# An attention and two-layer MLP kernel: finer steps in a hand-written order list, its first part written anew

## The chip, the core and the metric

The kernel runs on one core of one Trainium2 chip. The metric is device time in microseconds (us). The kernel before takes 994.7 us in the median of three runs, 994.26 to 994.94.

## The reference

Three stages follow each other. A recurrent attention with decay runs over 768 steps for 4 batches and 8 heads of 48 channels; its output, 3072 tokens of 384 channels, goes through a gated MLP with 1536 inner channels, and that through an MLP with 2048 inner channels and a squared ReLU.

```python
for t in range(S):
    cur = np.einsum('bhd,bhe->bhde', u[None] * kt, vt)
    y[:, :, t] = np.einsum('bhd,bhde->bhe', rt, state + cur)
    state = wt[:, :, :, None] * state + np.einsum('bhd,bhe->bhde', kt, vt)
x = y                                   # as 3072 tokens x 384
gate = 1.0 / (1.0 + np.exp(-(x @ w_gate)))
x = (gate * (x @ w_val)) @ w_out        # 1536 inner channels
h = np.maximum(x @ w_in, 0.0)           # 2048 inner channels
out = (h * h) @ w_out2
```

The weights reach the kernel as 64-bit floating point numbers, everything else as 32-bit ones.

## The kernel before

**Chunks.** The attention is cut into 24 chunks of 128 tokens (6 per batch, taken batch by batch within each of the 6 positions). Four chunks are one group of 512 tokens. Each chunk goes through stages that the code names by letters. S (`st_scan`) forms decay products by two scans on VectorE and scales r and k by them (L368 to L380). B and R (`st_bonus`, `st_bonus2`) form the diagonal term; GpSimd spreads it into a score tile (L424). A (`st_a`) computes scores on TensorE (L451) and copies the upper triangle into the score tile on VectorE (L454). K (`st_kt`) transposes k on TensorE (L435) and ScalarE copies it out. D decays the state, U (`st_u`) adds the chunk's k-v product to it (L486, L493). Y (`st_y`) computes the output (L466, L472) and splits it into a high and a low part, xh and xl, the input of the MLP. G checks the decay's range on ScalarE; L loads a later chunk.

**The low-high pairs.** A 32-bit operand goes to TensorE as a high half (a cast on ScalarE, L74) and a low half (a subtraction on VectorE, L75). One product is three matmuls: high by high, high weight by low x, low weight by high x (`mm3`, L499 to L501).

**Slots.** The first MLP is cut into 12 tiles of 128 inner channels. A slot is one tile for one group: P projects for the gate into bank gv0 (9 matmuls) and takes a sigmoid on ScalarE; Q projects for the value into gv1 and multiplies on VectorE (L534), and ScalarE casts the product to its high half (L535); l forms its low half gl on VectorE (L539); M multiplies by the output weights into three banks acc (9 matmuls).

**Weight tiles.** Each of the 12 tiles arrives as 1152 KB of 64-bit numbers (raw) and is converted on the chip. `Unit` does this in three ticks (T): a shifts (L195), b joins the low word (L204) and runs a range check on ScalarE (L209), c joins the high word (L215) and runs a second check on ScalarE (L220). The tick after c starts with the split into high and low half (`d`, which casts on ScalarE in L74 and subtracts in L75), and then begins the next tile. `Stream` counts the ticks and issues the loads, four tiles ahead.

**The order.** The scheduler leaves the order as written. A list of letters, `START`, holds the order up to the end of the second group (24 slots); `STEADY` repeats per chunk afterwards. Each letter appends its instructions to the queue of each engine it uses, and each engine works through its queue in order. W n puts n filler matmuls on TensorE (L639, no result used). Z, ahead of the first slot, limits the banks that chunk stages rotate through from eight to the three named rot. The loads of chunks 0 to 3, of their tokens (`load_tok`) and of the first three weight tiles are issued ahead of the list, all on SyncE's queue.

Of the kernel before, what the change touches and what calls it, by code (L numbers as in the profile page):

```python
# [5 lines left out]
F32 = mybir.dt.float32  # L6
# [9 lines left out]
DM = H * D  # L16
# [22 lines left out]
    S0 s0 R0 B1 A0 T B2 R1 K0 W10 S1 T U0 S2 G1 Y0 T W6 A1 K1 R2 T W14 A2 G0 L4 K2 T U1 B3 S3 B4 Y1 L5 W20 R3  # L39
    U2 Y2 W10 A3 G3 K3 T W2 Y3 T U3 R4 P0 T Q0 S4 P1 Q1 D4 l0 B5 W4 K4 T A4 T W3 U4 G4 Y4 G2 l1 T S5 T Z W7  # L40
    P2 M0 T T M1 T Q2 l2 T W1 P3 K5 R5 G5 W7 Q3 W3 P4 T D5 T A5 L6 l3 B6 M2 M3 T T T Q4 l4 U5 T P5 Y5 Q5 T P6
    T S6 M4 T Q6 D6 T R6 l5 T l6 W8 K6 P7 L7 M5 A6 T T Q7 M6 T B7 l7 U6 T P8 Q8 T l8 T S7 W4 P9 Y6 T M7 G6 Q9
    R7 D7 T M8 P10 K7 T A7 L8 Q10 l9 U7 T Y7 M9 l10 G7 P11 B8 Q11 M10 l11 M11 S8 P12 Q12 L9 P13 Q13 R8 l12 D8
    A8 P14 M12 l13 Y8 K8 G8 S9 M13 Q14 U8 B9 P15 D9 T l14 L10 B10 Q15 R9 M14 S10 P16 l15 G9 Q16 A9 M15 Y9 P17
    D10 l16 K9 Q17 M16 U9 R10 l17 P18 A10 K10 L11 B11 Q18 P19 M17 Q19 l18 P20 U10 l19 G10 M18 S11 Q20 D11 P21
    Y10 l20 R11 L12 M19 Q21 M20 K11 P22 l21 S12 G11 Q22 P23 A11 M21 U11 l22 Y11 Q23 B12 R12 M22 L13 l23
# [4 lines left out]
    D K P t Q B+ t l G M P t Q A S+ t l t U M P Y t t Q L t l M t R+  # L51
# [16 lines left out]
EARLY = 8  # L68
VW = 64
# [8 lines left out]
def rwkv_moe(tc, att, tok, vt, u, uc, w1, w2, out):  # L78
# [3 lines left out]
    with ExitStack() as ctx:  # L82
# [77 lines left out]
        class Unit:  # L160
# [99 lines left out]

        def w1_unit(f, note=None):
# [11 lines left out]
            return Unit(3 * DM, w1[f], raw, h, split, note)  # L273
# [5 lines left out]
        s1 = Stream([w1_unit(f, f) for f in range(F1)], 4)  # L279
# [175 lines left out]

        def st_y(i, xh, xl, n):
            d = chunk[i]
            a, v, am, s = d["a"], d["v"], d["am"], block[i % 2]
            py = bank().rearrange("p (a b) -> p a b", b=128)
# [16 lines left out]
            cs = slice(C * n, C * n + C)  # L476
            split_hi_lo(nc, xh[:, :, cs], xl[:, :, cs], py[:, 0:KT])

        def st_u(i):
# [3 lines left out]
            pu = bank()  # L483
# [6 lines left out]
            s = state[d["b"]]  # L490
# [87 lines left out]
        xs = {0: new_x(0)}  # L578
# [13 lines left out]
        def to_x(i):  # L592
            st_y(i, *xs[i // 4], i % 4)

        def load(i):
# [4 lines left out]
            S=lambda i: half(i, 0), s=lambda i: half(i, 1), D=st_decay, G=st_guard, A=st_a, K=st_kt, B=st_bonus, R=st_bonus2,  # L600
            Y=to_x, U=st_u, L=load,
        )
        slots = {}

        def slot(i):
            if i not in slots:
                g, f = i // F1, i % F1
                if f == 0 and g + 1 < NG:
                    xs[g + 1] = new_x(g + 1)
                elif f == 0:  # L610
                    xs[g + 1] = load_x2(0)
# [3 lines left out]
        def st_p(i):  # L615
            if i < F1:
                s1.until(3 * i + 3)
            slot(i).proj(0)
            slot(i).sig()

        def st_q(i):
            slot(i).proj(1)
            slot(i).prod()
# [10 lines left out]
        def warm_up(n):  # L634
# [7 lines left out]
            W=warm_up, P=st_p, Q=st_q, l=lambda i: slot(i).low(), M=st_m, Z=banks,  # L642
            T=lambda i: s1.tick(), t=lambda i: s2.tick(), r=lambda i: refill.tick(), F=lambda i: st_flag(),
# [4 lines left out]
        def steady(g):  # L648
# [3 lines left out]
            seq, n = [], dict(P=F1 * g, Q=F1 * g, l=F1 * g, M=F1 * g - 1)  # L652
# [13 lines left out]
        def last():  # L666
            seq = []
            for f in range(F1):
                k = F1 * (NG - 1) + f
                r = ["r", 0] if f else []  # L670
                seq += ["P", k] + (["F", 0] if f == 1 else []) + ["Q", k] + r + ["l", k] + r
# [247 lines left out]
```

## Time and profile before

| what | value |
|---|---|
| median of three runs | 994.7 us |
| the profiled execution, its own time | 995.02 us |
| its span | 993.3 us |
| TensorE busy | 965.6 us |
| VectorE busy | 534.3 us |
| ScalarE busy | 366.8 us |
| GpSimd busy | 102.6 us |
| mean granted TensorE clock | 0.995 |

Engines are PE (TensorE), PEld (its weight loads, beside PE), DVE (VectorE), ACT (ScalarE), POOL (GpSimd) and SP (SyncE, which issues the DMAs). Busy times of engines overlap, so they don't add up to the span. Names in rows are those of the program: a chunk's input is `a`, its tokens `t`, a weight tile before conversion `raw`, during it `h`, after it `w`. An idle time in brackets belongs to the instruction behind it, and the arrow names what that instruction waited for.

### The profile page before, as it was taken

How to read it: one execution, taken by the hardware profiler on the slowest of the kernel's cores; microseconds unless marked ns; L12 is line 12 of the kernel's file. 1: busy time of each engine (PE TensorE's matmuls, PEld its weight loads, DVE VectorE, ACT ScalarE, POOL GpSimd, SP SyncE). 2: the span in 40 equal slices, each digit the busy share in tenths (PEclk: the TensorE clock that was granted, in tenths of full speed). 3: DMA queues.
4: the chain of work that ended last, by engine and by line, in shares of the span. 5: the costliest groups of instructions: out<-in, count | busy, mean ns of one | idle time of the engine just before them, and what ended most of it. 6: DMA issues, size and time to landing. Idle time of an engine off the chain costs nothing.

```text
span 993.3 us, 14960 instructions
## 1 busy us (share of the span) xinstructions
PE 965.6 (97%) x6157; PEld 820.3 (83%) x6157; DVE 534.3 (54%) x802; ACT 366.8 (37%) x687; POOL 102.6 (10%) x100
## 2 busy tenths in 40 slices
PE   4989999999999999999999999999999999999997
PEld 4766778878888888888888889999999999999997
DVE  6998985645777677777632323333333333333332
ACT  1656563322433333333324433333233323332322
POOL 1100011111112111111104530000000000000000
PEclk9899999999999999999999999999999999999999
DMA  9951112204443443345303320010010100100001
GB/s 256 339 226 34 36 56 87 83 28 134 132 161 127 147 161 126 127 159 168 109 20 118 99 85 30 1 64 1 1 64 1 35 30 1 65 1 1 32 1 36
DMA packets 29724, 83.91 MB, mean 84 GB/s; under 512 B 3456, under 2 KB 15072, under 8 KB 28112
## 3 DMA queue, kind: packets, MB, share of 16 engines
q1 hardware_dynamic: 29504, 82.68, 25.6%
q8 instruction: 50, 0.82, 0.4%
q14 instruction: 26, 0.21, 0.1%
q10 hardware_dynamic: 144, 0.20, 0.1%
HBM read 67.13 MB, written 15.73 MB: 83 GB/s over the span
## 4 chain that ended last, share of the span: by engine, by line
PE 87%; DVE 7%; ACT 2%; DMA 1%; issue 1%; SPq 0%; ACTq 0%; DVEq 0%
PE gv L499 12%; PE gv L501 12%; PE gv L500 12%; PE acc L722 5%; PE acc L720 5%; PE acc L721 5%; PE acc L499 5%; PE acc L500 5%; PE acc L501 5%; PE rot L500 3%; PE rot L501 3%; PE rot L499 3%; PE rot L451 2%; PE rot L722 2%; PE rot L721 2%; PE rot L720 2%
## 5 line engine op out<-in xcount | busy, mean ns | idle before, releaser
L499 PE MATMUL gv<-xh,w 128*128 128x512 f32 x432 | 172.6, 399 | 1.3 <-DVE xl L75 0.8
L501 PE MATMUL gv<-xh,w 128*128 128x512 f32 x432 | 168.8, 391 | 1.2 <-DVE w L75 1.2
L500 PE MATMUL gv<-xl,w 128*128 128x512 f32 x432 | 168.5, 390 | 0.0
L711 DVE TENSOR_TENSOR sig<-sig 128x512 f32<-128x512 f32 x96 | 66.4, 692 | 175.0 <-ACT sig L710 175.0
L534 DVE TENSOR_TENSOR sig<-gv,sig 128x512 f32<-128x512 f32 x72 | 49.6, 688 | 116.8 <-PE gv L501 103.7
L499 PEld LDWEIGHTS gv<-xh,w 128*128 128x128 f32 x432 | 81.1, 188 | 21.6 <-issue 3.0
L501 PEld LDWEIGHTS gv<-xh,w 128*128 128x128 f32 x432 | 81.1, 188 | 20.1 <-DVE w L75 2.9
L720 PE MATMUL acc<-w,gh 128*128 128x384 f32 x288 | 96.7, 336 | 0.0
L721 PE MATMUL acc<-w,gh 128*128 128x384 f32 x288 | 96.6, 335 | 0.0
L535 ACT CAST gh<-sig 128x512 fp32r<-128x512 f32 x72 | 44.7, 621 | 138.4 <-DVE sig L534 138.4
L500 PEld LDWEIGHTS gv<-xl,w 128*128 128x128 f32 x432 | 81.2, 188 | 15.6
L74 ACT CAST gh<-sig 128x512 fp32r<-128x512 f32 x96 | 59.6, 621 | 78.9 <-DVE sig L711 78.9
L500 PE MATMUL acc<-gl,w 128*128 128x512 f32 x216 | 84.6, 392 | 2.6 <-DVE gl L539 2.6
L499 PE MATMUL acc<-gh,w 128*128 128x512 f32 x216 | 86.5, 400 | 0.0
L501 PE MATMUL acc<-gh,w 128*128 128x512 f32 x216 | 84.2, 390 | 0.0
L529 ACT ACTIVATE sig<-gv 128x512 f32<-128x512 f32 x72 | 43.0, 597 | 94.3 <-PE gv L501 93.4
L710 ACT ACTIVATE sig<-rot 128x512 f32<-128x512 f32 x48 | 28.6, 597 | 100.7 <-PE rot L501 97.7
L424 POOL TENSOR_SCALAR_AFFINE_SELECT am<-a 128x1024 f32<-128x1024 f32 x22 | 28.5, 1294 | 353.4 <-DVE a L415 236.6
L539 DVE TENSOR_TENSOR gl<-sig,gh 128x512 fp32r<-128x512 f32 x72 | 52.6, 730 | 19.2 <-ACT gh L535 19.2
L710 ACT ACTIVATE sig<-gv 128x512 f32<-128x512 f32 x48 | 28.7, 598 | 77.6 <-PE gv L501 76.1
L501 PE MATMUL rot<-xhs,w 128*128 128x512 f32 x144 | 56.5, 392 | 0.0
L501 PE MATMUL gv<-xhs,w 128*128 128x512 f32 x144 | 56.5, 392 | 0.0
(149 smaller groups left out, 1832.6 us busy)
## 6 DMA issues: line engine op xcount, KB each, us to landing
a<-in_att SPq DMA_DIRECT2D x23, 675.5 KB, 5.7
raw<-in_w SPq DMA_DIRECT2D x12, 1152.0 KB, 12.4
raw<-in_w SPq DMA_DIRECT2D x32, 384.0 KB, 4.0
t<-in_tok SPq DMA_DIRECT2D x16, 640.0 KB, 6.5
w2f<-h SPq DMA_DIRECT2D x32, 192.0 KB, 2.1
h<-w2f SPq DMA_DIRECT2D x32, 192.0 KB, 2.5
x2d<-x2o SPq DMA_DIRECT2D x18, 256.0 KB, 2.1
x2r<-x2d SPq DMA_DIRECT2D x6, 768.0 KB, 4.4
```

The costliest lines, as they stand in the source:

```text
L74: nc.scalar.copy(hi, src)
L499: nc.tensor.matmul(o, w_hi, x_hi, start=start, stop=False)
L500: nc.tensor.matmul(o, w_hi, x_lo, start=False, stop=False)
L501: nc.tensor.matmul(o, w_lo, x_hi, start=False, stop=stop)
L534: nc.vector.tensor_tensor(out=self.s[:, :n], in0=gv[1][:, :n], in1=self.s[:, :n], op=ALU.mult)
L535: nc.scalar.copy(self.gh[:, :n], self.s[:, :n])
L539: nc.vector.tensor_tensor(out=self.gl[:, :n], in0=self.s[:, :n], in1=self.gh[:, :n].bitcast(F32), op=ALU.subtract)
L710: nc.scalar.activation(r, self.h, AF.Relu)
L711: nc.vector.tensor_tensor(out=r, in0=r, in1=r, op=ALU.mult)
L720: nc.tensor.matmul(o, self.gh[:, cs], hi, start=b0, stop=False)
L721: nc.tensor.matmul(o, self.gh[:, cs], lo, start=False, stop=False)
L722: nc.tensor.matmul(o, self.gl[:, cs], hi, start=False, stop=b1)
```

## The change

**Steps.** A, Y and U are split: A keeps the matmuls, C copies the triangle; Y keeps the matmuls, X splits into high and low; U keeps the matmuls, V updates the state. Q is split into Q (matmuls) and q (product and cast). The conversion of a weight tile is split further: ticks a, b, c stay, but the second check is its own letter N, the high half H and the low half E. `Slots` takes the place of `Stream` for these tiles; it no longer ends a conversion by itself.

**Loads.** Chunk 1 moves ahead of chunk 0's tokens, and chunk 2 ahead of chunk 1's, chunk 3 ahead of chunk 2's.

**Lists.** `START` is written anew with these letters. `STEADY` gets the new letters right behind the old ones (`Q q`, `A C`, `U V`, `Y X`).

```diff
-    S0 s0 R0 B1 A0 T B2 R1 K0 W10 S1 T U0 S2 G1 Y0 T W6 A1 K1 R2 T W14 A2 G0 L4 K2 T U1 B3 S3 B4 Y1 L5 W20 R3
...
+    W33 S0 s0 B1 S1 W6 W15 R0 A0 C0 B2 S2 W8 W2 K0 R1 G0 Y0 U0 K1 L4 T V0 R2 U1 V1 X0 G1 A1 T C1 W3 N0 W15 W5 W3
...
-    D K P t Q B+ t l G M P t Q A S+ t l t U M P Y t t Q L t l M t R+
+    D K P t Q q B+ t l G M P t Q q A C S+ t l t U V M P Y X t t Q q L t l M t R+
...
+            def small(self):
+                n, junk = slice(self.note, self.note + 1), self.lo.bitcast(F32)
+                nc.scalar.activation(junk, junk, AF.Relu, bias=1.0, scale=-1.0 / TINY, accum_out=out_s[:, n])
...
-                if self.note is not None:
-                    n, junk = slice(self.note, self.note + 1), self.lo.bitcast(F32)
-                    nc.scalar.activation(junk, junk, AF.Relu, bias=1.0, scale=-1.0 / TINY, accum_out=out_s[:, n])
...
+        class Slots:
...
+            def tick(self):
+                k, part = divmod(self.k, 3)
+                if k >= len(self.u):
+                    return
+                self.k += 1
+                if part == 0:
+                    self.fetch(k + 1)
+                    self.u[k].a()
+                    self.fetch(k + self.ahead)
+                elif part == 1:
+                    self.u[k].b()
+                else:
+                    self.u[k].c()
...
+            def low(self):
+                if self.e < self.k // 3:
+                    self.u[self.e].low()
+                    self.e += 1
...
+            def high():
+                unit.w = w_slot(f)
+                nc.scalar.copy(flat(unit.w[:, 0]), unit.h)
+
+            def low():
+                hi, lo = flat(unit.w[:, 0]), flat(unit.w[:, 1])
+                nc.vector.tensor_tensor(out=lo, in0=unit.h, in1=hi.bitcast(F32), op=ALU.subtract)
...
-        s1 = Stream([w1_unit(f, f) for f in range(F1)], 4)
+        s1 = Slots([w1_unit(f, f) for f in range(F1)], 4)
...
-            pa = [bank().rearrange("p (a b) -> p a b", b=128) for _ in range(2)]
+            pa = d["pa"] = [bank().rearrange("p (a b) -> p a b", b=128) for _ in range(2)]
...
+        def st_mask(i):
+            d = chunk[i]
             for j in range(2):
                 m = mask.bitcast(I32).unsqueeze(1).to_broadcast([128, NP, C])
-                nc.vector.copy_predicated(d["am"][j], m, pa[j])
...
+        def st_x(i):
+            xh, xl = xs[i // 4]
+            cs = slice(C * (i % 4), C * (i % 4) + C)
+            split_hi_lo(nc, xh[:, :, cs], xl[:, :, cs], chunk[i]["py"][:, 0:KT])
...
         load_att(0, True)
+        load_att(1)
+        nc.sync.dma_start(up, uc)
         load_tok(0)
-        nc.sync.dma_start(up, uc)
-        load_att(1)
+        load_att(2, tag=f"w{F1 - 1}")
         load_tok(1)
         s1.fetch(1)
-        load_att(2, tag=f"w{F1 - 1}")
+        load_att(3, tag=f"w{F1 - 3}")
         load_tok(2, tag=f"w{F1 - 2}")
-        load_att(3, tag=f"w{F1 - 3}")
         load_tok(3, tag=f"w{F1 - 4}")
```

Where the instructions stand is shown at three places. The first is VectorE's queue just ahead of the first slot, before the change. Rows `rk` and `cum` to `a` are a chunk's diagonal term, scans and scaling (`a_341` is chunk 4, in the changed kernel `a_329`), `h` is a step of a weight tile's conversion (`raw_166` is tile 1), `w` its low half, `xl` the low half of a chunk's output.

```order
L399 TENSOR_TENSOR rk_369<-a_341 112x512
L75 TENSOR_TENSOR xl_173<-rot_123,xh_172 128x3x128
L75 TENSOR_TENSOR xl_173<-acc_118,xh_172 128x3x128
L454 COPY_PREDICATED room<-mask,acc_119 128x512
L454 COPY_PREDICATED room<-mask,acc_120 128x512
L215 SCALAR_TENSOR_TENSOR h<-raw_166,h 128x1152
L75 TENSOR_TENSOR xl_173<-gv_122,xh_172 128x3x128
L75 TENSOR_TENSOR w_496<-h,w_496 128x1152
```

And there in the changed kernel:

```order
L454 TENSOR_TENSOR rk_508<-a_329 112x512
L423 SCALAR_TENSOR_TENSOR cum<-a_329,inj 112x520
L428 TENSOR_SCALAR inj<-cum 112x4
L429 RECIPROCAL inj<-inj 112x4
L430 SCALAR_TENSOR_TENSOR cum<-a_329,inj 112x520
L435 TENSOR_TENSOR a_329<-a_329,cum 112x1024
L325 TENSOR_TENSOR w_533<-h,w_533 128x1152
L79 TENSOR_TENSOR xl_173<-gv_121,xh_172 128x3x128
L79 TENSOR_TENSOR xl_173<-acc_119,xh_172 128x3x128
L223 SCALAR_TENSOR_TENSOR h<-raw_166,h 128x1152
```

Chunk 4's scans and scaling and tile 0's low half now stand ahead of the last two xl; tile 1's last step stands behind them, and tile 1's low half further down.

The second place is VectorE's queue at the conversion of tile 3 (`raw_209`, `w_695`), before the change. `sig` is the product of a slot, `gl` its low half.

```order
L215 SCALAR_TENSOR_TENSOR h<-raw_209,h 128x1152
L75 TENSOR_TENSOR w_695<-h,w_695 128x1152
L195 TENSOR_SCALAR h<-raw_313 128x1152
L204 SCALAR_TENSOR_TENSOR h<-raw_313,h 128x1152
L215 SCALAR_TENSOR_TENSOR h<-raw_313,h 128x1152
L534 TENSOR_TENSOR sig<-gv_122,sig 128x512
L539 TENSOR_TENSOR gl<-sig,gh 128x512
L75 TENSOR_TENSOR w_729<-h,w_729 128x1152
```

In the changed kernel tile 3 is `raw_335` and `w_738`, and `a_651` is chunk 5:

```order
L223 SCALAR_TENSOR_TENSOR h<-raw_335,h 128x1152
L199 TENSOR_SCALAR h<-raw_431 128x1152
L600 TENSOR_TENSOR sig<-gv_122,sig 128x512
L423 SCALAR_TENSOR_TENSOR cum<-a_651,inj 112x520
L428 TENSOR_SCALAR inj<-cum 112x4
L429 RECIPROCAL inj<-inj 112x4
L430 SCALAR_TENSOR_TENSOR cum<-a_651,inj 112x520
L435 TENSOR_TENSOR a_651<-a_651,cum 112x1024
L325 TENSOR_TENSOR w_738<-h,w_738 128x1152
L600 TENSOR_TENSOR sig<-gv_122,sig 128x512
L208 SCALAR_TENSOR_TENSOR h<-raw_431,h 128x1152
L605 TENSOR_TENSOR gl<-sig,gh 128x512
```

The low half stood right behind the last conversion step; now the next tile's first step, a product and chunk 5's scans stand between the two.

The third place is SyncE's queue, which issues the loads, at its start, before the change (`t` are a chunk's tokens, `raw_156` is tile 0, `a_152` and `a_158` are chunks 1 and 2).

```order
L325 DMA a_144<-in_att 112x512
L337 DMA t_149<-in_tok 128x512
L566 DMA up<-in_uc 112x8
L327 DMA a_152<-in_att 112x1544
L337 DMA t_154<-in_tok 128x512
L176 DMA raw_156<-in_w 128x2304
L327 DMA a_158<-in_att 112x1544
```

In the changed kernel chunk 1 is `a_149`, chunk 2 `a_154`, chunk 3 `a_160`, tile 0 `raw_158`:

```order
L380 DMA a_144<-in_att 112x512
L382 DMA a_149<-in_att 112x1544
L632 DMA up<-in_uc 112x8
L392 DMA t_152<-in_tok 128x512
L382 DMA a_154<-in_att 112x1544
L392 DMA t_156<-in_tok 128x512
L180 DMA raw_158<-in_w 128x2304
L382 DMA a_160<-in_att 112x1544
```

Chunk 1 moved ahead of chunk 0's tokens, and chunk 2 ahead of chunk 1's tokens and of tile 0.

## Rows read from the trace of the kernel before

**Rows 1.** Page, busy us, share of the span, instructions of each engine

```profile
PE 965.6 (97%) x6157; PEld 820.3 (83%) x6157; DVE 534.3 (54%) x802; ACT 366.8 (37%) x687; POOL 102.6 (10%) x100
```

**Rows 2.** Stretches: us, busy us by engine (count), granted clock, DMA share, GB/s

```profile
3.04:47.06 44.02, 32.27 (x372) 26.57 (x372) 36.23 (x50) 17.33 (x39) 4.88 (x4) 0.92 1.02 314
47.37:147.95 100.58, 93.50 (x720) 72.17 (x719) 90.00 (x106) 63.00 (x114) 8.77 (x6) 1.00 0.27 93
147.95:900.00 752.05, 752.05 (x4623) 641.51 (x4622) 377.83 (x600) 258.64 (x490) 87.03 (x78) 1.00 0.24 78
```

**Rows 3.** TensorE waits, 47.3 to 148 us: total, times, longest

```profile
PE acc L500 <- DVE gl L539: 2.6, 2, 1.3
PE gv L501 <- DVE w L75: 1.2, 4, 0.7
```

**Rows 4.** Chain of waits, 60 to 100 us, shares by line

```profile
by line: ACT w L74 14.4%; DVE w L75 13.7%; DVE h L204 13.2%; ACT raw L220 13.0%; DVE h L195 10.9%; ACT raw L209 10.4%; issue 6.1%; DVE h L215 3.2%; DVE cum L375 3.1%; DVE a L380 3.1%; DVE cum L368 2.9%; DVE gl L539 1.5%; DVE sig L534 1.5%; 
```

**Rows 5.** VectorE waits, 0 to 47.3 us

```profile
DVE rk L399 <- DMA a<-in_att: 4.9, 2, 2.6
DVE h L195 <- DMA raw<-in_w: 1.5, 1, 1.5
```

**Rows 6.** VectorE waits, 47.3 to 148 us

```profile
DVE w L75 <- ACT w L74: 5.0, 7, 1.3
DVE gl L539 <- ACT gh L535: 2.7, 2, 1.4
DVE am L454 <- PE rot L451: 1.5, 1, 1.5
```

**Rows 7.** VectorE in order of time: start, us, instruction [idle before]

```profile
11.30 1.26 DVE L399 TENSOR_TENSOR rk<-a 112x512 f32<-112x512 f32 x1 [2.59 <-DMA a<-in_att]
...
44.70 1.34 DVE L215 SCALAR_TENSOR_TENSOR h<-raw,h 128x1152 int32<-128x1152 int32 x1
46.50 0.56 DVE L75 TENSOR_TENSOR xl<-gv,xh 128x384 fp32r<-128x384 f32 x1 [0.45 <-ACT xh L74]
...
52.88 1.23 DVE L368 TENSOR_TENSOR_SCAN cum<-a,inj 112x520 f32<-112x520 f32 x1
...
55.84 1.23 DVE L380 TENSOR_TENSOR a<-a,cum 112x1024 f32<-112x1024 f32 x1
...
73.41 1.36 DVE L75 TENSOR_TENSOR w<-h,w 128x1152 fp32r<-128x1152 f32 x1 [1.28 <-ACT w L74]
```

**Rows 8.** TensorE in order of time

```profile
47.37 0.48 PE L499 MATMUL gv<-xh,w 128*128 128x512 f32 x1
...
57.12 0.61 PE L435 MATMUL rot<-ident,a 112*128 112x112 f32 x4 [0.85 <-DVE a L380]
57.66 1.16 PE L451 MATMUL acc<-a 48*128 48x128 f32 x16
...
63.16 0.94 PE L639 MATMUL rot<-ident 128*128 128x256 bf16 x7
...
93.55 0.67 PE L486 MATMUL rot<-t,kt 128*64 128x48 f32 x16
...
147.95 0.40 PE L499 MATMUL gv<-xh,w 128*128 128x512 f32 x1
```

**Rows 9.** Stretches ahead of the first projection

```profile
0.00:30.00 30.00, 17.45 (x141) 14.72 (x142) 20.33 (x32) 8.65 (x18) 4.11 (x14) 0.91 0.94 285
20.00:24.00 4.00, 0.36 (x6) 0.36 (x8) 3.86 (x6) 0.00 (x0) 0.00 (x0) 1.00 1.03 339
26.00:28.00 2.00, 2.00 (x12) 1.82 (x11) 1.86 (x5) 1.97 (x8) 0.00 (x0) 0.50 1.04 435
30.00:32.00 2.00, 2.00 (x20) 1.47 (x19) 1.99 (x4) 1.21 (x2) 1.60 (x1) 0.70 1.02 424
```

**Rows 10.** Page, DMA issues: count, KB each, us to landing

```profile
a<-in_att SPq DMA_DIRECT2D x23, 675.5 KB, 5.7
raw<-in_w SPq DMA_DIRECT2D x12, 1152.0 KB, 12.4
```

More of the change, by code (lines that the diff above doesn't have):

```diff
@@ L68 @@
 EARLY = 8
+AFTER = 12
 VW = 64
@@ L259, in until, with __init__, fetch, small @@
                     self.tick()
+        class Slots:
+            def __init__(self, units, ahead):
+                self.u, self.n, self.k, self.e, self.ahead = units, 0, 0, 0, ahead
+            def fetch(self, n):
+                while self.n < min(n, len(self.u)):
+                    self.u[self.n].load()
+                    self.n += 1
+            def tick(self):
[11 more added lines that the diff above has]
+                    self.u[k].c()
+            def small(self, k):
+                self.u[k].small()
+            def high(self, k):
+                self.u[k].high()
+            def low(self):
+                if self.e < self.k // 3:
+                    self.u[self.e].low()
+                    self.e += 1
+            def until(self, n):
+                assert self.e >= n
         def w1_unit(f, note=None):
@@ L272, in w1_unit @@
             h = lambda: flat(sb.tile([128, 3, DM], F32, name="h", tag="h", bufs=2))
-            return Unit(3 * DM, w1[f], raw, h, split, note)
+            unit = Unit(3 * DM, w1[f], raw, h, split, note)
+            def high():
[4 more added lines that the diff above has]
+                nc.vector.tensor_tensor(out=lo, in0=unit.h, in1=hi.bitcast(F32), op=ALU.subtract)
+            unit.high, unit.low = high, low
+            return unit
         def w2_unit(i):
@@ L451, in st_a, with st_y @@
                     nc.tensor.matmul(pa[j][:, p], a[r, p, 1], a[r, p, 0], start=True, stop=True)
+        def st_mask(i):
+            d = chunk[i]
             for j in range(2):
                 m = mask.bitcast(I32).unsqueeze(1).to_broadcast([128, NP, C])
-                nc.vector.copy_predicated(d["am"][j], m, pa[j])
-        def st_y(i, xh, xl, n):
+                nc.vector.copy_predicated(d["am"][j], m, d["pa"][j])
+        def st_y(i):
             d = chunk[i]
             a, v, am, s = d["a"], d["v"], d["am"], block[i % 2]
-            py = bank().rearrange("p (a b) -> p a b", b=128)
+            py = d["py"] = bank().rearrange("p (a b) -> p a b", b=128)
             first = d["c"] == 0
@@ L482, in st_u @@
                 return
-            pu = bank()
+            pu = d["pu"] = bank()
             for h in range(H):
@@ L489, in st_u, with st_state @@
                 )
-            s = state[d["b"]]
+        def st_state(i):
+            d = chunk[i]
+            if d["c"] == NC_ - 1:
+                return
+            s, pu = state[d["b"]], d["pu"]
             un = pu[0:PR, 0 : NP * D].rearrange("p (a b) -> p a b", b=D)
@@ L599, in rwkv_moe @@
         stage = dict(
-            S=lambda i: half(i, 0), s=lambda i: half(i, 1), D=st_decay, G=st_guard, A=st_a, K=st_kt, B=st_bonus, R=st_bonus2,
-            Y=to_x, U=st_u, L=load,
+            S=lambda i: half(i, 0), s=lambda i: half(i, 1), D=st_decay, G=st_guard, A=st_a, C=st_mask, K=st_kt, B=st_bonus,
+            R=st_bonus2, Y=st_y, X=st_x, U=st_u, V=st_state, L=load,
         )
         slots = {}
+        order = [(g, f) for g in range(NG) for f in range(F1)]
         def slot(i):
             if i not in slots:
-                g, f = i // F1, i % F1
-                if f == 0 and g + 1 < NG:
+                g, f = order[i]
+                if i == AFTER:
+                    xs[2] = new_x(2)
+                elif g >= 2 and f == 0 and g + 1 < NG:
                     xs[g + 1] = new_x(g + 1)
-                elif f == 0:
+                elif g >= 2 and f == 0:
                     xs[g + 1] = load_x2(0)
@@ L615, in st_p @@
         def st_p(i):
-            if i < F1:
-                s1.until(3 * i + 3)
+            s1.until(order[i][1] + 1)
             slot(i).proj(0)
             slot(i).sig()
-        def st_q(i):
-            slot(i).proj(1)
-            slot(i).prod()
         def st_m(i):
@@ L641, in rwkv_moe @@
         stage.update(
-            W=warm_up, P=st_p, Q=st_q, l=lambda i: slot(i).low(), M=st_m, Z=banks,
-            T=lambda i: s1.tick(), t=lambda i: s2.tick(), r=lambda i: refill.tick(), F=lambda i: st_flag(),
+            W=warm_up, P=st_p, Q=lambda i: slot(i).proj(1), q=lambda i: slot(i).prod(), l=lambda i: slot(i).low(), M=st_m, Z=banks,
+            T=lambda i: s1.tick(), E=lambda i: s1.low(), N=s1.small, H=s1.high, t=lambda i: s2.tick(), r=lambda i: refill.tick(), F=lambda i: st_flag(),
             f=lambda i: st_flag2(),
```

27 lines of the change are left out of this document (13 added, 14 removed).

## Prediction

> **What bounds the kernel now.** I read the page first, then the stretches, the waits of TensorE and VectorE, the chain, and last both engines in order of time. The page gives TensorE 97% of the span [rows 1], so the only time to be won is where it is idle or does filler. The stretches say where that is. From 147.95 us, where the last of the 12 slots of the first token group begins, to 900 us TensorE is busy 752.05 of 752.05 us; from 47.37, where the first projection begins, to 147.95 it is busy 93.50 of 100.58 us; and before 47.37 it has done only chunk work and filler [rows 2, 8]. What stands behind the order list is the same instruction for instruction on all five engines in both programs, so the 845 us after 147.95 cost what they cost now, and the question is when that point is reached.
>
> TensorE waits there for VectorE: for the low half of a gated product (gl, L539), for the low half of a weight tile (w, L75), for a scaled chunk [rows 3]. The chain from 60 to 100 us runs through the conversion of the weight tiles and hardly touches TensorE: casts on ScalarE (L74), the steps on VectorE (L195, L204, L215, L75), two checks on ScalarE (L209, L220) [rows 4]. VectorE is busy 36.23 of the 44.02 us from its first scan to the end of the last xl ahead of the first projection, and 90.00 of the next 100.58 [rows 2]. It is the second full engine, and its own waits count: 4.9 us for chunk inputs and 1.5 for the first weights [rows 5], later 5.0 for the cast of a weight tile, 2.7 for that of a product, 1.5 for scores [rows 6]. The cast wait is built into the order: the low half is queued right behind the step that the cast needs, as at 73.41 us, with 1.28 us idle [rows 7].
>
> **The change part by part.** No arithmetic is added; the same instructions stand in another order, plus 31 filler matmuls (130 for 99). Of these, 126 stand ahead of the first projection (62 before) and 4 behind it (37 before).
>
> *Up to the first projection.* In both programs it waits for the xl of all four first chunks. VectorE's work up to that point is today's 36.23 us [rows 2], plus chunk 4's scans and scaling, which now come first (52.88 to 57.0, 4.1 us), less the last step of weight tile 1, which now comes after (44.70, 1.34 us) [rows 7]: 39.0 us. Its idle time today is 44.02 - 36.23 = 7.8 us. The loads of chunks 1 and 2 move ahead of the tokens of chunk 0 and of the first weights, and tile 0 is converted after chunk 2 rather than between chunks. Chunk 1's wait is 2.59 us (at 11.30). One 256 KB token load no longer stands ahead of it; at the 285 GB/s of the first 30 us [rows 9] that is 0.9 us, so 1.7 us of wait stay. Chunk 2 then has chunk 1's five steps as cover, tile 0 another five, and I cost both waits at nothing; the 0.45 before the xl at 46.50 goes too, since the last two xl now stand behind tile 0's low half. With 0.9 us of small gaps 2.6 us of idle stay. So the last xl ends at 3.04 + 39.0 + 2.6 = 44.6 and the first projection starts 0.3 later as today, at 44.9: **2.5 us earlier**, with chunk 4's scores and transposes already done.
>
> Two bounds for this. If chunk 1's wait goes too, and operations that no longer start after a wait run closer together, as the ones at 52.88 to 57.0 do (1.24 + 0.17 + 0.18 + 1.24 + 1.23 in 4.1), it is 42.5. If instead chunk 4's input is late, every later row of VectorE's queue is: with itself and what stands ahead of it, five chunk loads, four of tokens (256 KB), three weight tiles and one of 192 KB, 8.24 MB must have moved [rows 10], which at 285 GB/s have moved at 28.9 us; with the 5.7 us that such a load takes to land it is there at 34.6, and VectorE wants it at 44.6 less the 7 us of the rows between, 37.6. It is in time by 3 us, not by more; a tenth less bandwidth makes it even. I take 46.5 as the late end.
>
> *From there to slot 11.* TensorE's work today is 93.50 us [rows 2]. The filler that goes is 33 matmuls at 0.94 / 7 = 0.13 us, 4.4 us. Chunk 4's transposes (0.61) and scores (1.16) moved ahead, one state update (0.67) came in [rows 8]: -1.1. That leaves 88.0 us. VectorE's work is 90.00 - 4.1 + 1.3 = 87.2 us from the last xl to the low half of tile 11. So the two engines have the same amount of work between the same two points, and every wait on either shows. What stays of VectorE's 10.6 us of idle there (100.58 - 90.00)? High and low half of a tile are now two entries. For most tiles three or more other operations stand between the last conversion step and the low half, for tile 3 the next tile's first step, a product and a chunk's scans; only tiles 9 and 11 have two and one. So of the 5.0 us I keep 1.0. A product's low half stands one to nine operations behind its product: the 2.7 goes. Masks no longer follow the scores at once: 0.5 of 1.5 stays. I add 0.5 for a late chunk and keep the other 1.4 us of small gaps: 3.4 us. Tile 11 is then ready at 44.6 + 87.2 + 3.4 = 135.2; slot 11 needs it 0.5 us after its start, so it cannot start before 134.7, which is 44.9 + 88.0 + 1.8.
>
> TensorE has waits of its own besides. The split lets a PSUM bank be held from the scores to the masks and from the output to its x, while other work passes, and after the first projection three banks turn over. Chunk 6's scores take the bank that chunk 5's output filled, which VectorE empties only behind chunk 6's scans; chunk 7's transposes do the same with chunk 6. VectorE reaches these reads after 37.2 and 56.4 us of work from the last xl (the durations of its queue in the new order), TensorE reaches the transposes and scores after 37.2 and 57.2 us from the projection, which itself starts 0.3 after that xl. With 1 and 2 us of VectorE's idle by then, TensorE stands there for 0.7 and 0.9 us; the second holds a part of the first: 1.3 us in all. So slot 11 starts at 44.9 + 88.0 + 1.8 + 1.3 = 136.0 in place of 147.95, **11.95 us earlier**. Behind it, chunk 8's scores directly follow slot 11's projections and may wait a further microsecond; I count it in the range. Moved steps of ScalarE (checks, guards) go at nothing: it is busy 63.00 of 100.58 us [rows 2], and is hidden as long as no cast stands behind a sigmoid that waits for TensorE.
>
> The sum against the profiled execution's 995.02 us is 983.1. The median of the runs is 0.3 lower, 994.7, so I predict **982.8 us**.
>
> **The rivals.** *Both engines run full.* Projection at 42.5, bank and cast waits all covered, 0.5 us of idle: 42.5 + 88.0 + 0.5 = 131.0, 17 us earlier, 977.7. For it: enough operations stand between producer and consumer almost everywhere. Against it: two queues of 87 and 88 us that wait for each other a dozen times each.
>
> *VectorE's waits stay, under other names.* With all of its 10.6 us of idle kept, tile 11 is ready at 44.6 + 87.2 + 10.6 = 142.4, and slot 11 starts at 141.9: 6 us earlier, 988.6. With the late projection (46.5) it is 4.5 us, 990.2. For it: the amount of work is unchanged and ScalarE's queue is in order. Against it: 5.0 of the 10.6 us have a known cause which the new order removes.
>
> *The clock falls among the slots, and it is slower.* Filler no longer fills TensorE's waits behind the first projection. Today TensorE is busy 0.36 of the 4 us from 20 to 24 us, and then is granted 0.50 of its clock, the 1.2 GHz level; the stretch from 30 to 32 us shows 0.70, part of it at the 2.4 GHz level [rows 9]. One such episode costs the wait of 4 us, and half of the 7 us that follow it, 7.5 us. From two more than I count (12 + 2 us over 7.5) the kernel is slower than today; three make it 982.8 + 22 = 1005. The place would be a late chunk load, at which VectorE's whole queue stands, weights included. Against it: no wait of today behind 47.37 is over 1.3 us, with the clock at 1.00 throughout [rows 2, 3]. The Trainium skill's rule speaks for this rival (TensorE: Matmul & The Clock Gate, "Why this matters for your kernels": avoid idle gaps between bursts of matmuls, since one of them takes the array back to the lower clock). The trace agrees ahead of the projections, and shows no case behind them.
>
> *It does nothing that can be measured.* The list only trades places: what TensorE gains at the start it waits for later, because VectorE's sum is the bound. VectorE would need 15 to 17 us of idle between the two points, more than today's 10.6.
>
> **How the numbers follow.** My forecast, 979 to 986.5: 0.58. VectorE's waits stay, 986.5 to 991: 0.21. Both full, under 979: 0.13. Nothing measurable (about 0.2%, 2 us, is what this kernel's measurement can tell from no change): 0.04. Slower: 0.04. The range leaves out the nothing, the slower and the outer ends of the second and third: 977.5 to 989.5. Faster 0.92, same 0.04, slower 0.04.
>
> **What would show it.** First projection between 43.5 and 46; the wait of the weight tile's low half for its cast about 1 us in place of 5.0; TensorE's idle time from there to slot 11 about 3 us in place of 7.08; slot 11's start near 136, and the rest of the span as long as now. I am wrong if VectorE still idles 8 us or more between the two points, if a new wait for PSUM or for a chunk's load of over 2 us appears, or if TensorE shows idle time after slot 11.

## The result and the profile after

The changed kernel takes 978.68 us (median of 4 runs, 977.60 to 979.64), the kernel before 994.48 (4 runs, 992.52 to 994.94): a ratio of 0.9845, with a 95% interval of 0.9827 to 0.9862. It is 15.8 us faster. 982.8 was predicted, with a range of 977.5 to 989.5.

| us | before | predicted | after |
|---|---|---|---|
| first projection starts | 47.37 | 44.9 | 44.68 |
| from there to slot 11 | 100.58 | 91.1 | 88.18 |
| slot 11 starts | 147.95 | 136.0 | 132.86 |
| from there to the end of the span | 845.35 | as before | 844.94 |
| profiled execution | 995.02 | 983.1 | 979.64 |

The page of the changed kernel gives the busy time of each engine in us, its share of the span and the number of instructions [rows 1]:

```profile
PE 964.9 (99%) x6188; PEld 824.6 (84%) x6188; DVE 525.3 (54%) x802; ACT 365.7 (37%) x686; POOL 103.8 (11%) x100
```

TensorE's busy time is the same within a microsecond, with 31 more instructions. The span is 15.5 us shorter, and so the gain is idle time of TensorE. The stretches of the changed kernel show where (length, then the busy time of PE, PEld, DVE, ACT and POOL with their counts, granted clock, DMA share, GB/s) [rows 2]:

```profile
3.00:45.09 42.09, 39.66 (x437) 32.79 (x435) 37.83 (x55) 18.16 (x45) 6.43 (x5) 0.88 1.02 312
44.68:132.86 88.18, 85.79 (x681) 69.33 (x681) 86.45 (x102) 60.87 (x104) 13.71 (x9) 1.00 0.38 131
132.86:900.00 767.14, 766.75 (x4702) 656.22 (x4701) 376.64 (x609) 263.84 (x500) 82.15 (x76) 1.00 0.23 75
```

The second row is the one to compare. Idle time there is 88.18 - 85.79 = 2.39 us on TensorE (7.08 before) and 88.18 - 86.45 = 1.73 on VectorE (10.58 before). From slot 11 on TensorE is full, as before.

TensorE's waits in that stretch of the changed kernel (waiting line, what it waited for, us in total, times, longest) [rows 3]:

```profile
PE rot L506 <- DVE xl L79: 1.2, 1, 1.2
PE rot L506 <- DVE a L435: 0.7, 1, 0.7
PE rot L490 <- DVE xl L79: 0.4, 1, 0.4
```

The waits for gl and for the low half of a weight tile are gone. The first and the third row are new; in order of time (start, us, instruction, in brackets the idle time before it) they stand here [rows 8]:

```profile
44.68 0.49 PE L565 MATMUL gv<-xh,w 128*128 128x512 f32 x1
...
83.43 1.16 PE L506 MATMUL rot<-a 48*128 48x128 f32 x16 [1.23 <-DVE xl L79]
...
103.35 0.60 PE L490 MATMUL rot<-ident,a 112*128 112x112 f32 x4 [0.45 <-DVE xl L79]
...
132.86 0.39 PE L565 MATMUL gv<-xh,w 128*128 128x512 f32 x1
```

These are chunk 6's scores and chunk 7's transposes. Each waits until VectorE has read the output of the chunk before it out of the same bank.

VectorE's waits in the same stretch of the changed kernel [rows 6]:

```profile
DVE w L325 <- ACT w L321: 0.8, 3, 0.4
DVE gl L605 <- ACT gh L601: 0.4, 1, 0.4
```

And its waits from 0 to 48 us [rows 5]:

```profile
DVE xl L79 <- ACT xh L78: 2.2, 2, 1.3
DVE cum L423 <- DMA a<-in_att: 1.4, 1, 1.4
DVE rk L454 <- DMA a<-in_att: 1.3, 1, 1.3
```

The second row belongs to the first scan, which waits as long in both kernels. Behind it the waits for loads fell from 4.9 and 1.5 us to the 1.3 of the last row. The first row is a wait that the prediction did not have. The chain from 60 to 100 us has turned round [rows 4]:

```profile
by line: DVE w L325 13.1%; DVE h L208 10.7%; issue 10.0%; DVE h L223 9.4%; DVE cum L423 8.7%; DVE cum L430 6.3%; DVE gl L605 6.1%; DVE sig L600 6.0%; DVE am L512 5.2%; DVE h L199 5.1%; DVE inj L428 4.9%; ACT raw L217 3.5%; ACT w L321 2.9%; 
```

Before, three lines of ScalarE held 38% of it (a cast and two checks). Now they hold under 7%, and the chain runs from one VectorE instruction to the next. VectorE's queue still sets the end of this stretch, but it hardly stands still.

### The profile page after: what moved, and what is told of

It reads as the page before. It is cut to its first block, busy times and chain, and to the rows that moved or that the text cites. A ratio compares the mean times of both kernels' runs of the same rounds, so it can differ in the third digit from the quotient of the medians.

```text
span 977.8 us, 15032 instructions
## 1 busy us (share of the span) xinstructions
PE 964.9 (99%) x6188; PEld 824.6 (84%) x6188; DVE 525.3 (54%) x802; ACT 365.7 (37%) x686; POOL 103.8 (11%) x100
## 4 chain that ended last, share of the span: by engine, by line
PE 84%; DVE 10%; ACT 2%; issue 2%; DMA 1%; SPq 0%; ACTq 0%; DVEq 0%
PE gv L565 11%; PE gv L566 11%; PE gv L567 11%; PE acc L784 5%; PE acc L782 5%; PE acc L783 5%; PE acc L565 4%; PE acc L566 4%; PE acc L567 4%; PE rot L566 3%; PE rot L567 3%; PE rot L565 3%; PE rot L784 2%; PE rot L783 2%; PE rot L782 2%
## 5 line engine op out<-in xcount | busy, mean ns | idle before, releaser
L601 ACT CAST gh<-sig 128x512 fp32r<-128x512 f32 x72 | 44.6, 620 | 132.5 <-DVE sig L600 127.0
L479 POOL TENSOR_SCALAR_AFFINE_SELECT am<-a 128x1024 f32<-128x1024 f32 x22 | 27.8, 1266 | 327.8 <-DVE a L470 198.2
```

Of the source, the lines that this page charges most:

```text
L601: nc.scalar.copy(self.gh[:, :n], self.s[:, :n])
```

## The experiments

My theory: the gain is the time in which VectorE stood at an instruction whose producer on another engine was not done, while work that was ready stood behind it in its queue. The rivals: the first loads carry it; the filler that left TensorE carries it; or the amount of VectorE's work is all that counts, and the order nothing. Every ratio below is to the kernel before, in runs on the same chip; differences in us to the changed kernel (978.68) are across chips, on which the kernel before took 994.5 to 995.5 us.

### The first loads in the old order

```diff
 load_att(0)
-load_att(1); up
 load_tok(0)
-load_att(2)
+up
+load_att(1)
 load_tok(1)
...
+load_att(2)
 load_tok(2)
+load_att(3)
```

> The changed kernel with the old order of the first loads (chunk 0, its tokens, chunk 1, its tokens, tile 0, chunk 2), all else as changed. Theory 1 (the reason given in the prediction, only chunk 1's load gains, by one 256 KB token load): first projection 0.9 to 1.5 us later than the changed kernel's 44.68 us, total 979.5 to 980.5 us. Theory 2 (chunk 2 behind tile 0 matters too, since VectorE wants chunk 2 before tile 0 now): the wait of 2.3 us for chunk 2 comes back as well, first projection 3 us or more later, total 981.5 to 983 us.

Measured: 980.34 us, ratio 0.9846 (0.9825 to 0.9866). The first projection starts at 45.39 instead of 44.68, and the stretch to slot 11 takes 88.16 us instead of 88.18. So the order of the loads is worth 0.7 us of the 15.8 at the first projection (0.9 was the term for it), too little to show in the ratio. The list has the rest. The wait that theory 2 expected does come: VectorE waits 3.8 us for chunk inputs instead of 1.3, 3.0 of it at once. But its 2.2 us for the cast of xh are then gone, so that the projection hardly moves; with that wait removed by other means the loads could be worth more, which no run shows.

### The kernel before, without its late filler

```diff
-... l0 B5 W4 K4 T A4 T W3 U4 ... Z W7 P2 ... T W1 P3 K5 R5 G5 W7 Q3 W3 P4 ... W8 K6 ... W4 P9 ...
+... l0 B5 K4 T A4 T U4 ... Z P2 ... T P3 K5 R5 G5 Q3 P4 ... K6 ... P9 ...
```

> The kernel before without the 37 filler matmuls behind the first projection, all else as before. Theory 1 (as in the prediction's sum, filler is work that goes): 4.4 us less, 990 us. Theory 2 (it only filled waits for VectorE, which last as long without it): TensorE's idle time between first projection and slot 11 grows from 7.08 to 10 us or more, and the time stays within 1.5 us of 994.5. In either the clock could fall behind the first projection; by theory 2 it stays at 1.00, since no wait is over 2.5 us.

Measured: 996.54 us, ratio 1.0011 (0.9998 to 1.0024). Nothing is won. The stretch from the first projection to slot 11 in this kernel, and 25 us of it (columns as above):

```profile
47.97:148.47 100.50, 91.47 (x683) 71.42 (x683) 90.11 (x106) 63.05 (x114) 8.73 (x6) 0.97 0.27 94
...
75.00:100.00 25.00, 22.61 (x167) 17.62 (x168) 21.13 (x24) 17.29 (x30) 1.26 (x1) 0.93 0.09 33
```

TensorE has 37 instructions less than before and idles 9.03 us instead of 7.08; the stretch is as long as it was. The filler had only filled waits for VectorE. The granted clock is 0.93 from 75 to 100 us, where it was 1.00 with the filler, and even that adds nothing to the stretch, since TensorE is not what is waited for. Theory 2 is right on the time and wrong on the clock, which it expected to stay at 1.00.

### The low half back at its step

Only the place of H and E in the list changes (and for tiles 1, 3 and 4 that of the check N), for all but tiles 5, 7 and 11: they stand behind the last step and the check of their tile, ahead of the next tile's first step (tile 3 as the example).

```diff
-... T N3 L6 q1 H3 V3 S5 P2 E Q2 ...
+... T N3 H3 E T L6 q1 V3 S5 P2 Q2 ...
```

> The changed kernel with the cast and the low half of a weight tile back ahead of the next tile's first step, as in the kernel before (tiles 5, 7 and 11 stand so already), so that 0 to 1 us of VectorE work stands between last step and low half in place of 2 to 10 us. Theory 1 (the distance between last step and low half is what took the waits away): VectorE waits for casts of 5 us or more behind the first projection (0.8 in the changed kernel), total 982 to 986 us. Rival (the amount of work and the start decide, the waits move elsewhere): within 1.5 us of the changed kernel, 977.5 to 980 us.

Measured: 1004.26 us, ratio 1.0081 (1.0062 to 1.0100): the whole gain is gone, and more than theory 1 expected (982 to 986). VectorE's longest group of waits up to 180 us in this kernel (0.8 us in the changed kernel), and one of them in order of time:

```profile
DVE w L325 <- ACT w L321: 18.4, 10, 3.8
```

```profile
50.32 1.36 DVE L325 TENSOR_TENSOR w<-h,w 128x1152 fp32r<-128x1152 f32 x1 [1.27 <-ACT w L321]
```

What VectorE has to do between the last step of a tile and its low half was added up for each of the twelve tiles. Where it is nothing (seven tiles in this kernel) VectorE stands for 1.2 to 2.7 us each time; with 0.7 and 1.0 us of work it stands for 3.8 and 1.7; with 1.1 for 0.4, and with 5.8 and 6.1 us not at all. In the changed kernel this work is 1.1 to 6.0 us in tiles 1 to 11, and the three waits are 0.2, 0.2 and 0.4. So the distance is what the list has to give. It has to cover more than the cast itself (1.15 us on ScalarE): at the wait of 3.8 us two checks, a copy and another cast stand ahead of it in ScalarE's queue, and in the kernel before tile 11 waited 0.7 us with 3.3 us of work between.

Two of the ten waits lie ahead of the first projection, which starts at 51.24 instead of 44.68. From there to slot 11 it takes 106.70 us instead of 88.18, and VectorE idles 21.75 of them: about 16 for casts and 3.9 for TensorE. The granted clock is 0.91 there; how much a slower TensorE adds to these waits is not told apart here.

### The split steps joined again

Three kernels: C, X and V directly behind A, Y and U and also q behind Q; only q; only C, X and V. All else in the list keeps its place.

```diff
-... K0 R1 G0 Y0 U0 K1 L4 T V0 R2 U1 V1 X0 G1 A1 T C1 ... P0 Q0 Y4 T N2 L5 E B5 q0 ...
+... K0 R1 G0 Y0 X0 U0 V0 K1 L4 T R2 U1 V1 G1 A1 C1 T ... P0 Q0 q0 Y4 X4 T N2 L5 E B5 ...
```

> The changed kernel with the chunk stages and slots joined again: triangle copy right behind the scores (or behind the diagonal term, where that is later), split of the output right behind the output, state update right behind its matmuls, product right behind the value projection; conversions and loads as changed. Theory 1 (the split of conversions and the new list give the gain, the split of stages little): within 2.5 us of the changed kernel, 978 to 981 us, VectorE waiting 2 to 4 us more on TensorE. Rival (the split of stages carries it): 985 us or more.

Measured: 1016.46 us, ratio 1.0221 (1.0200 to 1.0241), 22 us slower than the kernel before. Theory 1 is out, and the loss is far over the rival's 985 us.

> The changed kernel with only the products joined again: product and its cast right behind the value projection in the list, all chunk stages split as changed. With everything joined the kernel took 1016 us, and VectorE waited 17.6 us for the value projection and 6.6 for sigmoids. Theory 1 (VectorE stands at a product that TensorE has not yet made, with work behind it): most of that comes back here, 990 to 1005 us, VectorE waiting 8 us or more for products. Rival (the chunk stages make it): within 3 us of the changed kernel.

Measured: 1005.85 us, ratio 1.0106 (1.0077 to 1.0135): theory 1, just above its range.

> The changed kernel with only the chunk stages joined (triangle copy, split of the output, state update right behind their matmuls); products stay apart, as changed. Everything joined was 38 us slower than the changed kernel, products alone 27 us. Theory 1 (a joined operation makes VectorE or ScalarE stand ahead of work that is ready): 985 to 995 us, with ScalarE's cast of the output and its copies of the state waiting for TensorE. Rival (the products made nearly all of it): 978 to 982 us.

Measured: 995.89 us, ratio 1.0011 (1.0001 to 1.0020): theory 1, again just above its range.

So the products alone cost 27 us against the changed kernel, the stages alone 17, and both 38, less than the sum. VectorE's waits, first in the kernel with the products joined, 43 to 150 us:

```profile
DVE sig L600 <- ACT sig L595: 8.5, 5, 2.4
DVE sig L600 <- PE gv L567: 6.3, 3, 3.2
```

Then with the stages joined, 0 to 140 us:

```profile
DVE xl L79 <- ACT xh L78: 12.8, 4, 5.5
```

One place of each in order of time, with the instruction behind it. Products joined:

```profile
49.61 0.69 DVE L600 TENSOR_TENSOR sig<-gv,sig 128x512 f32<-128x512 f32 x1 [1.85 <-ACT sig L595]
50.22 1.35 DVE L208 SCALAR_TENSOR_TENSOR h<-raw,h 128x1152 int32<-128x1152 int32 x1
```

Stages joined:

```profile
54.48 0.56 DVE L79 TENSOR_TENSOR xl<-rot,xh 128x384 fp32r<-128x384 f32 x1 [5.47 <-ACT xh L78]
54.95 1.35 DVE L208 SCALAR_TENSOR_TENSOR h<-raw,h 128x1152 int32<-128x1152 int32 x1
```

The changed kernel at the same first product:

```profile
48.45 1.34 DVE L208 SCALAR_TENSOR_TENSOR h<-raw,h 128x1152 int32<-128x1152 int32 x1
49.72 1.34 DVE L325 TENSOR_TENSOR w<-h,w 128x1152 fp32r<-128x1152 f32 x1
50.99 0.67 DVE L454 TENSOR_TENSOR rk<-a 112x512 f32<-112x512 f32 x1
51.59 0.67 DVE L600 TENSOR_TENSOR sig<-gv,sig 128x512 f32<-128x512 f32 x1
```

Joined, the conversion step (L208), whose data are there, stands behind a product that waits 1.85 us for a sigmoid. Split, the step runs first, and the product finds its sigmoid done. That is the theory, shown at both kinds of steps. What these kernels do not show is how good a list without splits could be: this one was written for split steps, and the kernel before, whose list was written for joined ones, is faster than the first two and about as fast as the third.

### No filler ahead of the first projection

```diff
-    W33 S0 s0 B1 S1 W6 W15 R0 A0 C0 B2 S2 W8 W2 K0 R1 G0 Y0 ... C1 W3 N0 W15 W5 W3 ...
+    S0 s0 B1 S1 R0 A0 C0 B2 S2 K0 R1 G0 Y0 ... C1 N0 ...
```

> The changed kernel without the 126 filler matmuls ahead of the first projection; the 4 behind it stay. Theory 1 (VectorE's queue sets the first projection, the filler only passes the time): first projection within 1 us of 44.68 us, total within 1.5 us of the changed kernel. Rival (it holds the clock up for the chunks' small matmuls and the first slots): with a granted clock of 0.5 in parts of the first 60 us, transposes, scores and outputs take twice as long, VectorE waits for them, and the first projection comes 3 to 6 us later, total 981.5 to 985 us. In the changed kernel the clock is 0.50 from 20 to 26 us all the same.

Measured: 979.18 us, ratio 0.9844 (0.9822 to 0.9865): the 126 filler matmuls are worth nothing that can be told. The first projection starts 1.1 us earlier (43.59), and VectorE no longer waits for the cast of xh ahead of it (2.2 us in the changed kernel): of its two parts there, 1.27 us end at 23.32, behind matmuls that ran at 0.50 of the clock, and 0.90 us end at 33.91, behind 26 filler matmuls that held TensorE for 4.58 us from 24.48. The stretch behind takes 88.20 us, as in the changed kernel. The clock ahead of the projection, in this kernel:

```profile
20.00:28.00 8.00, 7.09 (x102) 6.03 (x100) 7.97 (x9) 5.85 (x14) 2.06 (x1) 1.00 1.01 365
28.00:32.00 4.00, 1.33 (x12) 1.27 (x14) 3.86 (x6) 3.37 (x11) 0.87 (x1) 0.85 1.04 340
32.00:36.00 4.00, 3.08 (x43) 2.30 (x41) 4.00 (x8) 0.00 (x0) 1.88 (x1) 0.50 1.02 426
```

And in the changed kernel:

```profile
12.00:16.00 4.00, 2.78 (x30) 2.47 (x26) 3.90 (x6) 1.68 (x5) 1.61 (x2) 1.00 1.06 359
16.00:20.00 4.00, 3.66 (x54) 2.93 (x54) 3.90 (x7) 0.39 (x2) 0.40 (x1) 0.69 0.99 232
20.00:28.00 8.00, 8.00 (x58) 6.73 (x58) 6.69 (x9) 5.76 (x14) 1.15 (x1) 0.52 1.04 384
```

### Less work on VectorE, in both kernels

The step that joins the low word is left out for weight tiles 2 to 11, so that their weights lack their lowest bits.

```diff
-                i = self.h.bitcast(I32)
-                nc.vector.scalar_tensor_tensor(...)
+                if self.note is None or self.note < 2:
+                    i = self.h.bitcast(I32)
+                    nc.vector.scalar_tensor_tensor(...)
```

In the changed kernel:

> The changed kernel without the step that joins the low word (L208) in tiles 2 to 11, 10 operations of 1.27 us on VectorE; the tiles then lack their lowest bits. It asks how much of VectorE's 86.45 us of work between first projection and slot 11 still sets the time. Theory 1 (both engines are full there, TensorE idle 2.3 us): at most 2.5 us less than the changed kernel, 976 to 978.5 us. Rival (VectorE alone is the bound and TensorE would follow): 6 us less or more, below 973 us.

Measured: 975.10 us, ratio 0.9794 (0.9773 to 0.9815).

In the kernel before:

> The kernel before without the same step (L204) in tiles 2 to 11, 12.7 us of VectorE's work; the tiles lack their lowest bits. Theory 1 (its waits come from the order, and from VectorE's amount of work only where the queue is behind): TensorE's 7.08 us of idle between first projection and slot 11 fall to about 4, total 990 to 993 us. Rival (VectorE's amount of work is the bound before, so most of the step's time comes back): 7 us less or more, 988 us or below.

Measured: 986.40 us, ratio 0.9912 (0.9891 to 0.9934). The stretch from the first projection to slot 11, first of the changed kernel with less work, then of the kernel before with less work:

```profile
44.32:129.11 84.79, 84.79 (x681) 69.64 (x681) 76.54 (x93) 60.72 (x104) 13.58 (x9) 1.00 0.41 140
```

```profile
46.87:139.75 92.88, 90.59 (x719) 72.61 (x719) 76.28 (x96) 62.98 (x114) 7.98 (x6) 1.00 0.29 104
```

In the kernel before VectorE has 13.7 us less to do there and slot 11 comes 8.2 us earlier: the rival, by which the amount of VectorE's work was the bound too, was right there. In the changed kernel 9.9 us less bring 3.8 us, between the two expectations, and then TensorE is busy for the whole stretch. So VectorE's sum and its order both set the time before (the kernels with the low half back or with joined steps do the same work as the changed one, and lose 17 to 38 us); after the change TensorE alone lies only 3.4 us under the stretch (88.18 - 84.79).

### The r-k products on GpSimd

A try for a faster kernel: the one without early filler, with a VectorE product per chunk (L454, 0.68 us) handed to GpSimd, which is idle most of the time.

```diff
-                nc.vector.tensor_tensor(out=chunk[i]["rk"][:, ps], in0=a[:, ps, 0], in1=a[:, ps, 1], op=ALU.mult)
+                (nc.gpsimd if i else nc.vector).tensor_tensor(out=chunk[i]["rk"][:, ps], ..., op=ALU.mult)
```

> The changed kernel without the 126 early filler matmuls, and with the r-k products of chunks 1 to 7 (L454, 0.6 us each) on GpSimd in place of VectorE. Theory 1 (VectorE's work sets the first projection, and behind it a part of the time): first projection about 2 us earlier than the 43.59 us without early filler, total 974 to 977 us. Rival (GpSimd's reads hold VectorE back by as much as the 0.6 us that each product frees): first projection at 43 us or later, total 977 to 981 us.

Measured: 982.85 us, ratio 0.9882 (0.9865 to 0.9898), some 4 us slower than the kernel without early filler (979.18, on another chip). The first projection comes at 43.48, no earlier than 43.59, and the stretch grows from 88.20 to 93.52 us. VectorE's groups up to 137 us in this kernel (line, shape, count, busy us, mean ns):

```profile
L208 DVE SCALAR_TENSOR_TENSOR h<-raw,h 128x1152 int32<-128x1152 int32 x12 | 17.2, 1433 | 0.1
...
L430 DVE TENSOR_TENSOR_SCAN cum<-a,inj 112x520 f32<-112x520 f32 x7 | 10.1, 1441 | 0.2
L423 DVE TENSOR_TENSOR_SCAN cum<-a,inj 112x520 f32<-112x520 f32 x7 | 9.7, 1390 | 0.9 <-DMA a<-in_att 0.9
L435 DVE TENSOR_TENSOR a<-a,cum 112x1024 f32<-112x1024 f32 x7 | 9.4, 1342 | 0.7
...
L605 DVE TENSOR_TENSOR gl<-sig,gh 128x512 fp32r<-128x512 f32 x10 | 8.3, 831 | 0.4 <-ACT gh L601 0.4
```

The same groups in the kernel without early filler, from which this one differs by the move alone:

```profile
L208 DVE SCALAR_TENSOR_TENSOR h<-raw,h 128x1152 int32<-128x1152 int32 x12 | 16.9, 1408 | 0.0
...
L435 DVE TENSOR_TENSOR a<-a,cum 112x1024 f32<-112x1024 f32 x8 | 11.2, 1400 | 0.3
L423 DVE TENSOR_TENSOR_SCAN cum<-a,inj 112x520 f32<-112x520 f32 x8 | 10.9, 1369 | 0.0
L430 DVE TENSOR_TENSOR_SCAN cum<-a,inj 112x520 f32<-112x520 f32 x8 | 9.9, 1242 | 0.3
...
L605 DVE TENSOR_TENSOR gl<-sig,gh 128x512 fp32r<-128x512 f32 x10 | 7.2, 723 | 0.4 <-ACT gh L601 0.4
```

Most means are longer by 2 to 16%, one (L435) is shorter by 4%. The means hide that single instructions beside GpSimd's take up to 1.1 us more than the median of their kind while the others keep it; one such pair stands in the last section. Up to 130 us this excess is 8.6 us in all, for 5.0 without the move, so that 3.6 of the 4.2 us that seven products of 0.6 us free are lost again. The rival was right, and the loss is larger than it had it. VectorE's busy time in the stretch, 88.00 us, is higher than without the move (86.41). And TensorE waits 3.2 us for an xl that empties a bank, for which it does not wait at all without the move:

```profile
PE rot L506 <- DVE xl L79: 3.2, 1, 3.2
```

No version with the whole computation was measurably faster than the changed kernel.

## Why the prediction was right, and what was mis-sized

**The place.** Right: of the 15.5 us by which the span shrank, 2.69 lie ahead of the first projection and 12.40 between it and slot 11; the 845 us behind differ by 0.41.

**The first projection.** 44.9 predicted, 44.68 measured, but by luck: three errors cancel. VectorE's work up to the last xl is 37.8 us, not 39.0, and it idles 4.3 us, not 2.6: chunk 1's wait is 1.3 us (1.7 predicted), small gaps 0.8 (0.9), and a wait of 2.2 us for the cast of xh was costed at nothing. So the last xl ends at 45.09, not 44.6. And the projection starts 0.4 us ahead of that end, not 0.3 behind it: its first matmul reads the high half alone, and the first that reads xl starts at 45.14. The wait of 2.2 us goes with the early filler, as the run without it shows. Of the 1.2 us of missing work 0.8 is time in which VectorE was held up beside GpSimd (last section): 1.5 us of it ahead of the projection before, 0.7 after.

**The cast waits.** 5.0 us should have shrunk to 1.0; they are 0.8. The product's low half should have lost its 2.7; 0.4 is left. The reason given was right in kind, too narrow in words: of the seven tiles that waited before, only tile 3 had its low half directly behind its step, the others had 0.6 to 3.3 us of work between. With the distance taken away, the waits come back (18.4 us up to 180 us, 1004.26 us).

**The bank waits.** Predicted at chunk 6's scores (0.7 us) and chunk 7's transposes (0.9, the second holding a part of the first; 1.3 in all). Measured at these two places: 1.23 and 0.45, 1.7 in all. They were the only waits of TensorE that the change added; the third one left, 0.7 us for a scaled chunk, stands for 1.0 before (a row that rows 3 leave out).

**The step that failed in size: from the first projection to slot 11, "TensorE work", 88.0 us.** This term took before's busy 93.50 us for work. The kernel before with less VectorE work runs the same TensorE instructions there (719 recorded for 720) in 90.59 us of busy time, with 2.29 us of idle instead of 7.08. The granted clock is 1.00 in both, so 2.9 us of "busy" went with the waits. With 90.59 in the same sum, 90.59 - 4.4 - 1.1 = 85.1, against 84.79 in the changed kernel with less VectorE work, where TensorE never waits, and 85.79 in the changed kernel itself (87.4 in the two runs whose clock fell for a while, with the stretch as long). The credit of 4.4 us for 33 filler matmuls holds only in this sum; by itself, in the kernel before, the removal was worth nothing (996.54 us), because that filler covered waits.

**VectorE's side** was mis-sized as much, and the sum needs both: by it VectorE held slot 11 until 134.7 us however little TensorE had to do. From the last xl to the low half of tile 11 it has 85.65 us of work (87.2 predicted) and idles 1.73 (3.4 predicted), so tile 11 is ready at 132.47, not 135.2, and the 1.8 us that slot 11 was to wait for it did not come: no wait of TensorE for a weight tile is left in the stretch. Term by term slot 11 comes 0.2 us earlier by the first projection, 2.2 by TensorE's work, 1.8 by tile 11, and 1.1 later by TensorE's other waits (2.39 for 1.3): 132.86 for 136.0.

**The rivals.** *Both engines run full* gave 977.7 and, by its bound of 979, the median of 978.68 falls to it by 0.3 us: the forecast's own 979 to 986.5, given 0.58, was missed by as much. The rival's mechanism is not what happened: the first projection did not come at 42.5, and the bank waits were not covered. Its 88.5 us for the stretch meet the 88.18 by luck, with too much TensorE work and too little waiting. The forecast's mechanism with smaller terms on both engines gives the time. *VectorE's waits stay* is out: 1.73 of 10.58 us stay. *The clock falls* did not happen here (1.00 over the stretch), but its mechanism exists: the granted clock there was 0.97 without the late filler, 0.91 with the low half back at its step, and 0.92 to 0.97 in the three kernels with joined steps. In all of these TensorE waits longer, and how much of their time is the clock's share stays open. A short fall cost nothing: with the old loads and without early filler TensorE idles only 0.74 and 0.83 us in the stretch, the mean clock is 0.98, and the stretch takes 88.16 and 88.20 us. So the changed kernel does not owe its time to a clock of 1.00.

## What to carry to other kernels

When one engine's in-order queue sets the time of a stretch, look for instructions that wait for another engine while ready work stands behind them, split the step there, and put ready work between the two halves, enough for the producer and for what stands ahead of it in its own queue; in this list, which was written for split steps, taking that distance away cost 17 to 27 us for each kind of step, and the costs do not add up. Busy time in a stretch with many waits can hold some cost of the waits, so an estimate of what stays without them takes it too high (93.50 against 90.59 us). Filler that covers a wait can't be counted as a gain when it goes.

## What was not expected of the hardware

Filler did not keep the clock up for long. In the changed kernel TensorE is busy without a break from 2 to 14.8 us, with filler above all, and then stands 1.36 us for a mask. From 18 to 26 us it is granted 0.50 of its clock, the 1.2 GHz level, although it is busy again all the while; over 20 to 28 us that is 0.52 at 8.00 of 8.00 us busy. Without early filler it is busy for 7.09 of the same 8.00 us and is granted 1.00, the 2.4 GHz level. There the fall comes later, 0.50 from 32 to 36 us, behind a stretch of 4 us with only 1.33 busy. What the filler did buy lies at the very start: the same eight matmuls, in the changed kernel, without early filler, and in the changed kernel again while 0.50 was granted:

```profile
10.28 1.02 PE L467 MATMUL rot<-up,rk 112*128 112x2 f32 x8
```

```profile
10.28 1.84 PE L467 MATMUL rot<-up,rk 112*128 112x2 f32 x8 [10.28 <-DMA up<-in_uc]
```

```profile
19.78 1.73 PE L467 MATMUL rot<-up,rk 112*128 112x2 f32 x8
```

The profile gives a granted clock of 1.00 at the first two of these. By the durations that can't be right for the kernel without early filler: its next group of this kind takes 1.73 us too (at 14.87), and only the one at 20.39 us takes 1.06. So its clock column is not to be trusted up to there.

A short wait can be enough for a fall. A wait of TensorE for a scaled chunk (0.71 us without early filler, 0.65 with the old loads) is followed by 4 us at a granted clock of 0.62 (from 64 us) and 0.60 (from 66); the same wait of 0.71 us in the changed kernel is followed by 1.00 (from 65). Why it differs stays open.

Single VectorE instructions are held up while GpSimd works, beside its other instructions (L457, L458, L479) and not only beside the moved products. The moved product of chunk 1, the scan that starts beside it, and the same scan in the kernel without early filler:

```profile
9.53 1.26 POOL L454 TENSOR_TENSOR rk<-a 112x512 f32<-112x512 f32 x1 [6.96 <-DMA a<-in_att]
```

```profile
9.54 2.34 DVE L423 TENSOR_TENSOR_SCAN cum<-a,inj 112x520 f32<-112x520 f32 x1 [0.90 <-DMA a<-in_att]
```

```profile
10.52 1.23 DVE L423 TENSOR_TENSOR_SCAN cum<-a,inj 112x520 f32<-112x520 f32 x1
```

The scan takes its own 1.23 us and most of the product's 1.26. In the first 130 us of all twelve traces every VectorE instruction that is over 0.1 us longer than the median of its kind (kinds with three or more) overlaps one of GpSimd, in the kernel before too: 80 of them, 3 to 11 in each. Others overlap and keep their length, the split of an output (0.55 us) and most mask copies (0.72) among them.
